# Attention numerators moved into the FFN blocks, down weights streamed per block: a linear-attention plus SwiGLU kernel on one core

## The chip, the cores and the metric

The kernel runs on one core of a Trainium2 chip. The metric is the device time of one execution in microseconds (us). Executions of one kernel agree within 1%. Ratios are the mean time of one kernel's fast runs over that of the other kernel's fast runs of the same rounds, so they are not quite the ratio of the medians quoted beside them. Every "ratio" below is against the kernel before, measured on the same chip.

Words used: TensorE does matmuls, DVE is the vector engine, ScalarE the activation engine, PSUM the memory of the matmul accumulators (the kernels here use eight banks of it, 128 x 512 fp32 each). An "F tile" is a 128-wide slice of the FFN's hidden dimension; there are 36. A "block" is 512 tokens; there are four.

## The reference, cut to what matters

```python
# S = 2048 tokens, D = 576, 32 heads of 18, F = 4608, all bf16
xn  = layernorm(A_x)
q, k, v = heads(xn @ A_wqkv)
phi = lambda t: where(t > 0, t + 1, exp(t)) + 1e-6
kv  = phi(k)^T v          # per head, summed over all tokens
z   = phi(k) summed over tokens
o   = (phi(q) kv) / (phi(q) z + 1e-6)
out = A_x + o @ A_wo + (silu(xn @ B_w_gate) * (xn @ B_w_up)) @ B_w_down
```

Linear attention has one barrier: `kv` and `z` need all tokens before any `o` can be made. The kernel packs them, per group of seven heads, into a small matrix `R` of 126 + 7 columns: multiplying phi(q) by it gives numerators and denominators together.

## The kernel before

Four stages stand in this order: loads and the K/V stage over 16 token tiles; building R; a stage that makes q, numerators and normalised outputs of all tokens; and the FFN with the output projection, block by block. Cuts are marked with `# ...`.

```python
W_DOWN_EARLY_TILES = 6
ATTN_PROJ_AT = 2
ffn_sb = tile_pool(bufs=2)                    # sg, hT (3), ot
ps_x = tile_pool(bufs=3, space=PSUM)          # gate/up banks, shared with the attention "units"
# ... in the attention part: ps_tr 2 banks, ps_y 1, ps_kv 2
wd_a = wpool.tile([P, NFA, D], BF16)          # first 6 down-weight tiles, loaded early

def q_unit(blk, g):                           # phi(q) of one head group for 512 tokens
    pq = pq_buf[blk % 2]
    pu = unit_tile()
    for kt in range(KT):                      # 5 matmuls of 512 columns
        nc.tensor.matmul(pu[0:r, 0:SB], lhsT=wq_sb[...], rhs=xnT[:, kt, bs], ...)
    nc.scalar.activation(a[0:r, :], pu[0:r, 0:SB], ACT.Relu, scale=-1.0)
    nc.scalar.activation(e[0:r, :], a[0:r, :], ACT.Exp, scale=-1.0)
    nc.vector.scalar_tensor_tensor(pq[0:r, g, :], pu[0:r, 0:SB], 0.0, e[0:r, :],
                                   op0=ALU.max, op1=ALU.add)
# K/V stage: the five q units of block 0 are mixed in
early_q = [(0, g) for g in range(NG)]
for i in range(NST):
    transpose_in(i, xn_next)
    # ... layer_norm(i + 1)
    kv_tile(i)
    if i >= TPB and early_q:
        q_unit(*early_q.pop(0))
# ... R is built here
# attention stage: q of the next block, numerators, normalise, transpose, interleaved
for blk in range(NSB):
    for j in range(TPB):
        nd = nd_next
        if blk + 1 < NSB:
            for g in q_share(j):
                q_unit(blk + 1, g)
        # ... nd_next = numden_mm(...)          5 matmuls of 133 columns
        ot = normalize(blk, j, nd)              # DVE: 2 reciprocals, 2 products
        transpose_out(blk, j, ot)               # 5 transposes, one ScalarE copy to oT

def finish_block(blk):
    for j in range(TPB):
        ot = ffn_sb.tile([P, D], BF16, tag="ot")          # two buffers
        nc.vector.tensor_tensor(ot[:, 0:DMAIN], accm[j], xr[...], op=ALU.add)
        nc.vector.tensor_tensor(ot[:, DMAIN:D], acct[:, j, :], xr[...], op=ALU.add)
        nc.sync.dma_start(out2[rows, :], ot[:])
# FFN: per F tile 5 gate, 5 up matmuls, then the down matmuls of the tile before;
# attn_proj(blk) at F tile 2; accumulators take 5 PSUM banks
```

A scheduling layer reorders instructions by priority within the limits of data and buffers, so the order in the trace is near the program's, not equal to it.

## Time and profile before

| | before |
|---|---|
| median of 15 runs | 592.72 us (591.08 to 595.47) |
| profiled span | 592.2 us |
| TensorE busy | 95% |
| first K/V matmul to R | 62.1 us |
| first q unit after R to the last matmul | 507.5 us |
| last matmul to program end | 7.0 us |

The page of the kernel before: busy time and share of each engine, the granted TensorE clock in tenths over 40 slices, and the engines' shares of the chain of work that ended last.

```profile
span 592.2 us, 8308 instructions
...
PE 563.3 (95%) x3472; PEld 280.4 (47%) x3526; DVE 192.2 (32%) x397; ACT 163.5 (28%) x355; POOL 9.3 (2%) x54
...
PEclk7899999899999999999999999999999999999998
...
PE 88%; ACT 4%; DVE 3%; DMA 2%; issue 1%; SPq 1%; DVEq 0%
```

TensorE is the bound: 88% of the chain. (The 95% busy overstates it a little: matmuls overlap and their ends are modelled.) What is left to gain is where TensorE waits, which the stretches view of the same kernel shows. Columns: stretch in us from the start, its length, then busy time and instruction count of each engine, granted clock, DMA share, GB/s.

```profile
core 0: us, PE busy (x) PEld busy (x) DVE busy (x) ACT busy (x) POOL busy (x), PEclk, DMA share, GB/s
13.90:75.98 62.08, 58.57 (x495) 33.32 (x496) 43.88 (x117) 44.83 (x150) 0.16 (x2) 0.96 0.80 230
...
77.68:111.00 33.32, 28.39 (x225) 18.37 (x226) 28.20 (x76) 26.02 (x45) 0.00 (x0) 0.99 0.00 1
111.00:114.97 3.97, 3.75 (x17) 1.82 (x17) 1.23 (x4) 2.47 (x4) 0.00 (x0) 0.62 0.00 0
114.97:585.20 470.23, 467.30 (x2690) 222.73 (x2741) 109.14 (x170) 86.21 (x145) 0.00 (x0) 1.00 0.06 19
585.20:592.20 7.00, 0.00 (x0) 0.00 (x0) 2.36 (x7) 0.00 (x0) 0.00 (x0) 0.73 0.24 84
```

The FFN stretch is full. The attention stage from 77.68 us is not: 4.9 us idle on TensorE up to 111 us, then 4 us at a granted clock of 0.62. Its timeline, TensorE only (start, duration, instruction, count; in brackets the idle time before it and what ended it):

```profile
106.39 0.41 PE L343 MATMUL u<-R,pq 127*128 127x133 bf16 x4 [0.53 <-DVE pq L176]
107.18 0.23 PE L343 MATMUL u<-R,pq 127*128 127x133 bf16 x1 [0.38 <-DVE o L359]
...
109.01 0.28 PE L372 MATMUL pT<-ident,o 128*128 128x128 bf16 x2 [0.56 <-DVE o L359]
...
111.31 1.06 PE L468 MATMUL pg<-xnT,wg_sb 128*128 128x512 bf16 x2 [0.22 <-issue]
112.17 0.42 PE L372 MATMUL pT<-ident,o 128*128 128x128 bf16 x2
112.38 1.06 PE L468 MATMUL pg<-xnT,wg_sb 128*128 128x512 bf16 x2
```

The waits are for DVE: over the whole stage numerators wait 2.0 us for phi(q) (line 176) and transposes 1.8 us for the normalised product (line 359); one numerator waits for that product too (0.38). After them, from 110.6 to 114.0 us, the granted clock reads 0.50.

The end of the program, DVE only:

```profile
585.67 0.34 DVE L455 TENSOR_TENSOR ot<-acct,xr 128x64 bf16<-128x64 f32 x2
587.75 0.69 DVE L451 TENSOR_TENSOR ot<-accm,xr 128x512 bf16<-128x512 f32 x1 [1.74 <-DMA out_dram<-ot]
```

The third addition of the last block waits 1.74 us for an output transfer, because there are two output buffers.

### The profile page before, as it was taken

Reading aid. Unit: us, or ns where it says so; the run is one execution under the profiler, and the core shown is the slowest. Engines: PE = TensorE matmul, PEld = TensorE weight load, DVE = VectorE, ACT = ScalarE, POOL = GpSimd, SP = SyncE. Lnnn points to the kernel's source line nnn. Section 1 sums busy time; section 2 is a strip of 40 time slices with the busy share of each in tenths; the row PEclk is TensorE's granted clock in tenths of the full one; section 3 lists DMA queues with packets and bytes.
Section 4 is the critical chain, followed back from the end, with each engine's and each line's share of the span. In section 5 each row is a group of like instructions: output and inputs, shape, how many; then the busy total and the mean of one; then the engine's idle time right before and its main releaser. Section 6 shows DMA issues by size and latency. Waiting matters only on the chain.

```text
span 592.2 us, 8308 instructions
## 1 busy us (share of the span) xinstructions
PE 563.3 (95%) x3472; PEld 280.4 (47%) x3526; DVE 192.2 (32%) x397; ACT 163.5 (28%) x355; POOL 9.3 (2%) x54
## 2 busy tenths in 40 slices
PE   3999988899999999999999999999999999999995
PEld 2555555444444444444444444444444444444442
DVE  4777488512122223121222141221222412212223
ACT  1777778512212211122112211122122211221120
POOL 6000000000000000000000000000000000000000
PEclk7899999899999999999999999999999999999998
DMA  8999100180000000200000001000000010000001
GB/s 273 329 301 281 31 2 1 53 288 1 0 1 1 1 1 20 61 2 1 0 1 1 0 21 61 1 1 1 0 1 1 24 58 1 0 1 1 1 1 40
DMA packets 19482, 27.59 MB, mean 47 GB/s; under 512 B 1076, under 2 KB 14324, under 8 KB 19444
## 3 DMA queue, kind: packets, MB, share of 16 engines
q1 hardware_dynamic: 19444, 27.06, 15.0%
q8 instruction: 27, 0.44, 0.3%
q14 instruction: 11, 0.09, 0.1%
HBM read 24.70 MB, written 2.36 MB: 46 GB/s over the span
## 4 chain that ended last, share of the span: by engine, by line
PE 88%; ACT 4%; DVE 3%; DMA 2%; issue 1%; SPq 1%; DVEq 0%
PE pu L472 26%; PE pg L468 26%; PE accm L423 23%; PE u L268 5%; PE acct L429 4%; PE u L168 2%; DMA xo<-in_A_x_dram 1%; ACT e L277 1%; ACT a L275 1%; DMA out_dram<-ot 1%; ACT e L175 1%; ACT m L279 1%; DVE ot L451 1%; ACT a L173 1%; PE kvacc L292 1%
## 5 line engine op out<-in xcount | busy, mean ns | idle before, releaser
L477 DVE TENSOR_TENSOR hT<-pu,sg 128x512 bf16<-128x512 f32 x144 | 99.6, 691 | 363.0 <-PE pu L472 360.0
L475 ACT ACTIVATE sg<-pg 128x512 bf16<-128x512 f32 x144 | 86.0, 597 | 381.6 <-PE pg L468 362.9
L472 PE MATMUL pu<-xnT,wu_sb 128*128 128x512 bf16 x709 | 179.1, 379 | 0.8
L468 PE MATMUL pg<-xnT,wg_sb 128*128 128x512 bf16 x702 | 176.9, 381 | 0.9 <-issue 0.2
L423 PE MATMUL accm<-wd_b,hT 128*128 128x512 bf16 x459 | 129.7, 380 | 0.0
L472 PEld LDWEIGHTS <-wu_sb 128*128 128x128 bf16 x720 | 70.2, 98 | 84.1 <-issue 0.7
L429 PE MATMUL acct<-wd_b,hT 128*128 128x64 bf16 x480 | 92.5, 193 | 1.1
L468 PEld LDWEIGHTS <-wg_sb 128*128 128x128 bf16 x720 | 61.0, 98 | 68.5 <-issue 0.3
L423 PEld LDWEIGHTS <-hT 128*128 128x128 bf16 x576 | 56.4, 98 | 68.2 <-DVE hT L477 0.2
L429 PEld LDWEIGHTS <-hT 128*128 128x128 bf16 x576 | 56.0, 98 | 17.5 <-issue 0.4
L268 PE MATMUL u<-wkv_sb,xnT 128*128 128x504 bf16 (+1 forms) x320 | 44.6, 296 | 7.1 <-DVE xnT L256 7.0
L268 PEld LDWEIGHTS <-xnT 128*128 128x128 bf16 x320 | 22.4, 101 | 28.0 <-DVE xnT L256 7.8
L423 PE MATMUL accm<-wd_a,hT 128*128 128x512 bf16 x92 | 26.9, 380 | 0.1
L168 PE MATMUL u<-xnT,wq_sb 128*126 128x512 bf16 (+1 forms) x100 | 24.7, 380 | 0.4 <-DVE pq L176 0.4
L423 PE MATMUL accm<-wo_sb,xo 126*128 126x512 bf16 (+1 forms) x80 | 20.2, 380 | 0.0
L429 PE MATMUL acct<-wd_a,hT 128*128 128x64 bf16 x96 | 17.0, 193 | 0.2
L275 ACT ACTIVATE a<-u 128x504 bf16<-128x504 f32 (+1 forms) x32 | 13.1, 410 | 14.0 <-PE u L268 13.9
L176 DVE SCALAR_TENSOR_TENSOR pq<-u,e 126x512 bf16<-126x512 f32 (+1 forms) x20 | 13.8, 689 | 5.6 <-ACT e L175 4.9
L429 PE MATMUL acct<-wo_sb,xo 126*128 126x64 bf16 (+1 forms) x80 | 15.3, 192 | 0.0
L280 DVE SCALAR_TENSOR_TENSOR pk<-e,m 128x504 bf16<-128x504 bf16 (+1 forms) x32 | 13.1, 451 | 5.8 <-ACT e L277 5.8
L238 DVE BATCH_NORM_STATS2 st<-xo 128x6 f32<-128x288 bf16 x32 | 12.6, 442 | 6.8 <-DMA xo<-in_A_x_dram 6.8
L168 PEld LDWEIGHTS <-wq_sb 128*126 128x126 bf16 (+1 forms) x100 | 11.8, 132 | 6.2 <-issue 0.8
(61 smaller groups left out, 231.1 us busy)
## 6 DMA issues: line engine op xcount, KB each, us to landing
wg_sb<-in_B_w_gate_dram SPq DMA_DIRECT2D x4, 1152.0 KB, 14.6
wu_sb<-in_B_w_up_dram SPq DMA_DIRECT2D x4, 1152.0 KB, 14.9
wd_b<-in_B_w_down_dram SPq DMA_DIRECT2D x5, 864.0 KB, 6.6
xr<-in_A_x_dram SPq DMA_DIRECT2D x4, 576.0 KB, 4.6
out_dram<-ot SPq DMA_DIRECT2D x16, 144.0 KB, 2.2
xo<-in_A_x_dram SPq DMA_DIRECT2D x1, 1152.0 KB, 9.3
wg_sb<-in_B_w_gate_dram SPq DMA_DIRECT2D x8, 144.0 KB, 14.1
wu_sb<-in_B_w_up_dram SPq DMA_DIRECT2D x8, 144.0 KB, 13.4
```

The costliest lines, as they stand in the source:

```text
L168: nc.tensor.matmul(pu[0:r, 0:SB], lhsT=wq_sb[:, kt, g * GW:g * GW + r], rhs=xnT[:, kt, bs], start=(kt == 0), stop=(kt == KT - 1),)
L176: nc.vector.scalar_tensor_tensor(pq[0:r, g, :], pu[0:r, 0:SB], 0.0, e[0:r, :], op0=ALU.max, op1=ALU.add)
L238: nc.vector.bn_stats(st[:, c, :], x_all[:, i, c * BN_CH:(c + 1) * BN_CH])
L268: nc.tensor.matmul(pu[:, 0:w], lhsT=xnT[:, kt, tok], rhs=wkv_sb[:, kt, c0:c0 + w], start=(kt == 0), stop=(kt == KT - 1),)
L275: nc.scalar.activation(a[:, 0:w], pu[:, 0:w], ACT.Relu, scale=-1.0)
L280: nc.vector.scalar_tensor_tensor(pk[:, g0:g1, 0:r], e[:, 0:w].rearrange("p (g c) -> p g c", c=r), PHI_EPS, m[:, 0:w].rearrange("p (g c) -> ...
L423: nc.tensor.matmul(st["accm"][j][:, 0:DMAIN], lhsT=lhsT, rhs=rhs_full[:, 0:DMAIN], start=st["first_main"][j], stop=last,)
L429: nc.tensor.matmul(st["acct"][:, j, :], lhsT=lhsT, rhs=rhs_full[:, DMAIN:D], start=st["first_tail"], stop=last, skip_group_check=True,)
L468: nc.tensor.matmul(pg[:, 0:SB], lhsT=wg_sb[:, kt, fs], rhs=xnT[:, kt, bs], start=(kt == 0), stop=(kt == KT - 1))
L472: nc.tensor.matmul(pu[:, 0:SB], lhsT=wu_sb[:, kt, fs], rhs=xnT[:, kt, bs], start=(kt == 0), stop=(kt == KT - 1))
L475: nc.scalar.activation(sg[:], pg[:, 0:SB], ACT.Silu)
L477: nc.vector.tensor_tensor(hT[:], pu[:, 0:SB], sg[:], op=ALU.mult)
```

## The change

The intent: no stage in which TensorE waits for normalisation. All 20 q units run in one go after R and all phi(q) stay in SBUF; numerators, normalisation and transposes become twelve small steps per block, one in every second F tile of the FFN, where other engines have time. To pay for the memory, the down weights are no longer resident but streamed in chunks of six tiles (three buffers), once per block. PSUM pays too: gate/up have two banks instead of three, and one bank serves the steps. Output buffers go from two to four. The output projection moves from F tile 2 to after the last step (F tile 25). Lines that begin with `#`, here and in the cuts below, stand for code left out.

```diff
-W_DOWN_EARLY_TILES = 6
+W_DOWN_CHUNK = 6
+W_DOWN_BUFS = 3
-ATTN_PROJ_AT = 2
+EPI_START = 1
-    ps_x = ctx.enter_context(tc.tile_pool(name="ps_x", bufs=3, space=PSUM))
+    ps_x = ctx.enter_context(tc.tile_pool(name="ps_x", bufs=2, space=PSUM))
-    wd_a = wpool.tile([P, NFA, D], BF16, name="wd_a")
+    pq_all = [wpool.tile([P, NG, SB], BF16, name=f"pq{b}") for b in range(NSB)]
+    o_buf = [wpool.tile([P, NG, P], BF16, name=f"o{j}") for j in range(2)]
-        ps_y = ... bufs=1 ...
+        ps_y = ... bufs=2 ...
                 kv_tile(i)
-                if i >= TPB and early_q:
-                    q_unit(*early_q.pop(0))
 # ... R is built
-        # the interleaved attention stage
+        for blk in range(NSB):
+            for g in range(NG):
+                q_unit(blk, g)
+        wdp = bctx.enter_context(tc.tile_pool(name="wdp", bufs=W_DOWN_BUFS))
+        ps_att = bctx.enter_context(tc.tile_pool(name="ps_att", bufs=1, space=PSUM))
+        # load_wd(q): one chunk of six down-weight tiles, two chunks ahead
+        # nd_step: 3 or 2 numerator matmuls, reciprocal, product; tr_step: 5 transposes, copy
-                ot = ffn_sb.tile([P, D], BF16, tag="ot")
+                ot = ffn_sb.tile([P, D], BF16, tag="ot", bufs=4)
+        spacing = max(1, (NFT - 6 - f_start) // n_steps)      # 2
                 prev = (blk, f, hT)
-                if f == attn_at:
-                    attn_proj(blk)
+                if pending and f >= f_start:
+                    n_emit = len(pending) if f == NFT - 1 else int((f - f_start) % spacing == 0)
+                    for _ in range(n_emit):
+                        pending.pop(0)()
+                    if not pending:
+                        proj_at = min(NFT - 1, f + 2)
+                if proj_at is not None and f >= proj_at:
+                    attn_proj(blk)
+                    proj_at = None
```

More of the change, by code (lines that the diff above doesn't have):

```diff
@@ L68 @@
     TPB = SB // P
-    NFA = min(W_DOWN_EARLY_TILES, NFT)
-    NFB = NFT - NFA
+    CH = min(W_DOWN_CHUNK, NFT)
+    NCH = (NFT + CH - 1) // CH
     DMAIN = min(D, BANK)
@@ L85 @@
     wu_sb = wpool.tile([P, KT, F], BF16, name="wu_sb")
-    wd_a = wpool.tile([P, NFA, D], BF16, name="wd_a")
     wo_sb = wpool.tile([P, NG, D], BF16, name="wo_sb")
     wq_sb = wpool.tile([P, KT, D], BF16, name="wq_sb")
+    ident = wpool.tile([P, P], BF16, name="ident")
+    R = wpool.tile([P, NG, NDW], BF16, name="R")
+    pq_all = [wpool.tile([P, NG, SB], BF16, name=f"pq{b}") for b in range(NSB)]
+    o_buf = [wpool.tile([P, NG, P], BF16, name=f"o{j}") for j in range(2)]
     def load_ktiled(dst, src, c0, c1, eng, d0=0):
@@ L104 @@
         ps_tr = actx.enter_context(tc.tile_pool(name="ps_tr", bufs=2, space=PSUM))
-        ps_y = actx.enter_context(tc.tile_pool(name="ps_y", bufs=1, space=PSUM))
+        ps_y = actx.enter_context(tc.tile_pool(name="ps_y", bufs=2, space=PSUM))
         ps_kv = actx.enter_context(tc.tile_pool(name="ps_kv", bufs=1, space=PSUM))
@@ L112, in unit_tile @@
             unit_ctr[0] += 1
-            pool, tag = (ps_y, "unit_y") if k % 4 == 3 else (ps_x, "unit")
+            pool, tag = (ps_y, "unit_y") if k % 2 else (ps_x, "unit")
             return pool.tile([P, BANK], F32, tag=tag, name=f"u{k}")
-        ident = apers.tile([P, P], BF16, name="ident")
         make_identity(nc, ident[:])
@@ L127 @@
         Rb = apers.tile([GW, NG, NDW], BF16, name="Rb")
-        R = apers.tile([P, NG, NDW], BF16, name="R")
-        pq_buf = [qpool.tile([P, NG, SB], BF16, name=f"pq{j}", bufs=1) for j in range(2)]
         def init_late_constants():
@@ L149, in init_late_constants @@
             nc.gpsimd.memset(Rb[:], 0.0)
-            for pqj in pq_buf:
+            for oj in o_buf:
+                nc.gpsimd.memset(oj[:, :, GW:P], 0.0)
+            for pqj in pq_all:
                 for g in range(NG):
@@ L164, in q_unit @@
             r = gsz[g]
-            pq = pq_buf[blk % 2]
+            pq = pq_all[blk]
             pu = unit_tile()
@@ L203 @@
                 load_ktiled(wu_sb, B_w_up, c0, c1, nc.sync, d0=c0)
-                if c == 0:
-                    nc.sync.dma_start(
-                        wd_a[:, :, :], B_w_down[0:NFA * P, :].rearrange("(ft p) d -> p ft d", p=P)
-                    )
             for g in range(NG):
@@ L296, in kv_tile @@
                     )
-            early_q = [(0, g) for g in range(NG)]
             xn_next = layer_norm(0)
@@ L304 @@
                 kv_tile(i)
-                if i >= TPB and early_q:
-                    q_unit(*early_q.pop(0))
-            for bg in early_q:
-                q_unit(*bg)
             for g in range(NG):
@@ L325 @@
                 nc.any.tensor_copy(R[0:r + 1, g, :], pr[0:r + 1, 0:NDW])
-        with tc.tile_pool(name="a2", bufs=2) as a2:
-            o_buf = []
-            for j in range(2):
-                oj = a2.tile([P, NG, P], BF16, name=f"o{j}", bufs=1)
-                nc.gpsimd.memset(oj[:, :, GW:P], 0.0)
-                o_buf.append(oj)
-            ND_SPLIT = min(BANK // NDW, NG)
-            nd_parts = [(g0, min(NG, g0 + ND_SPLIT)) for g0 in range(0, NG, ND_SPLIT)]
-            def numden_mm(blk, j):
-                pq = pq_buf[blk % 2]
-                nd = []
-                for (g0, g1) in nd_parts:
-                    t = unit_tile()
-                    for g in range(g0, g1):
-                        r = gsz[g]
-                        nc.tensor.matmul(
-                            t[:, (g - g0) * NDW:(g - g0 + 1) * NDW],
-                            lhsT=pq[0:r + 1, g, j * P:(j + 1) * P], rhs=R[0:r + 1, g, :],
-                            start=True, stop=True,
-                        )
-                    nd.append(t)
-                return nd
-            def normalize(blk, j, nd):
-                i = blk * TPB + j
-                ot = o_buf[i % 2]
-                for (g0, g1), t in zip(nd_parts, nd):
-                    n = g1 - g0
-                    v3 = t[:, 0:n * NDW].rearrange("p (g c) -> p g c", c=NDW)
-                    rden = a2.tile([P, ND_SPLIT, HG], F32, tag="rden")
-                    nc.vector.reciprocal(rden[:, 0:n, :], v3[:, :, GW:NDW])
-                    nc.vector.tensor_tensor(
-                        ot[:, g0:g1, 0:GW].rearrange("p g (h e) -> p g h e", e=Dh),
-                        v3[:, :, 0:GW].rearrange("p g (h e) -> p g h e", e=Dh),
-                        rden[:, 0:n, :].rearrange("p g (h o) -> p g h o", o=1)
-                        .to_broadcast([P, n, HG, Dh]),
-                        op=ALU.mult,
-                    )
-                return ot
-            def transpose_out(blk, j, ot):
-                i = blk * TPB + j
-                pT = ps_tr.tile([P, NG, P], BF16, tag="pT")
-                for g in range(NG):
-                    nc.tensor.transpose(pT[:, g, :], ot[:, g, :], ident[:])
-                nc.scalar.copy(oT[:, :, i * P:(i + 1) * P], pT[:])
-            def q_share(j):
-                return range((NG * j) // TPB, (NG * (j + 1)) // TPB)
-            nd_next = numden_mm(0, 0)
-            for blk in range(NSB):
-                for j in range(TPB):
-                    nd = nd_next
-                    if blk + 1 < NSB:
-                        for g in q_share(j):
-                            q_unit(blk + 1, g)
-                    if j + 1 < TPB:
-                        nd_next = numden_mm(blk, j + 1)
-                    elif blk + 1 < NSB:
-                        nd_next = numden_mm(blk + 1, 0)
-                    ot = normalize(blk, j, nd)
-                    transpose_out(blk, j, ot)
@@ L392 @@
+        for blk in range(NSB):
+            for g in range(NG):
+                q_unit(blk, g)
     with ExitStack() as bctx:
         bp = bctx.enter_context(tc.tile_pool(name="bp", bufs=1))
+        wdp = bctx.enter_context(tc.tile_pool(name="wdp", bufs=W_DOWN_BUFS))
         ps_acc = bctx.enter_context(tc.tile_pool(name="ps_acc", bufs=1, space=PSUM))
-        wd_b = None
-        if NFB:
-            wd_b = bp.tile([P, NFB, D], BF16, name="wd_b")
-            step = 6
-            for f0 in range(0, NFB, step):
-                f1 = min(NFB, f0 + step)
-                nc.sync.dma_start(
-                    wd_b[:, f0:f1, :],
-                    B_w_down[(NFA + f0) * P:(NFA + f1) * P, :].rearrange("(ft p) d -> p ft d", p=P),
-                )
@@ L407, in wd_tile, with load_wd @@
-        def wd_tile(f):
-            return wd_a[:, f, :] if f < NFA else wd_b[:, f - NFA, :]
+        ps_att = bctx.enter_context(tc.tile_pool(name="ps_att", bufs=1, space=PSUM))
+        wd_chunks = {}
+        n_chunks = NSB * NCH
+        def load_wd(q):
+            if q >= n_chunks or q in wd_chunks:
+                return
+            c = q % NCH
+            f0, f1 = c * CH, min(NFT, (c + 1) * CH)
+            t = wdp.tile([P, CH, D], BF16, tag="wd", name=f"wd{q}")
+            nc.sync.dma_start(
+                t[:, 0:f1 - f0, :],
+                B_w_down[f0 * P:f1 * P, :].rearrange("(ft p) d -> p ft d", p=P),
+            )
+            wd_chunks[q] = t
@@ new lines, in wd_tile, with nd_step @@
+        def wd_tile(blk, f):
+            q = blk * NCH + f // CH
+            load_wd(q)
+            return wd_chunks[q][:, f % CH, :]
+        for q in range(min(W_DOWN_BUFS - 1, n_chunks)):
+            load_wd(q)
+        ND_SPLIT = min(BANK // NDW, NG)
+        nd_parts = [(g0, min(NG, g0 + ND_SPLIT)) for g0 in range(0, NG, ND_SPLIT)]
+        def nd_step(blk, j, g0, g1):
+            pq = pq_all[blk]
+            ot = o_buf[(blk * TPB + j) % 2]
+            n = g1 - g0
+            t = ps_att.tile([P, BANK], F32, tag="att", name="nd")
+            for g in range(g0, g1):
+                r = gsz[g]
+                nc.tensor.matmul(
+                    t[:, (g - g0) * NDW:(g - g0 + 1) * NDW],
+                    lhsT=pq[0:r + 1, g, j * P:(j + 1) * P], rhs=R[0:r + 1, g, :],
+                    start=True, stop=True,
+                )
+            v3 = t[:, 0:n * NDW].rearrange("p (g c) -> p g c", c=NDW)
+            rden = ffn_sb.tile([P, ND_SPLIT, HG], F32, tag="rden")
+            nc.vector.reciprocal(rden[:, 0:n, :], v3[:, :, GW:NDW])
+            nc.vector.tensor_tensor(
+                ot[:, g0:g1, 0:GW].rearrange("p g (h e) -> p g h e", e=Dh),
+                v3[:, :, 0:GW].rearrange("p g (h e) -> p g h e", e=Dh),
+                rden[:, 0:n, :].rearrange("p g (h o) -> p g h o", o=1).to_broadcast([P, n, HG, Dh]),
+                op=ALU.mult,
+            )
@@ new lines, in tr_step, with epilogue_steps @@
+        def tr_step(blk, j):
+            i = blk * TPB + j
+            ot = o_buf[i % 2]
+            pT = ps_att.tile([P, NG, P], BF16, tag="att", name="oTp")
+            for g in range(NG):
+                nc.tensor.transpose(pT[:, g, :], ot[:, g, :], ident[:])
+            nc.scalar.copy(oT[:, :, i * P:(i + 1) * P], pT[:])
+        def epilogue_steps(blk):
+            steps = []
+            for j in range(TPB):
+                for (g0, g1) in nd_parts:
+                    steps.append(lambda j=j, g0=g0, g1=g1: nd_step(blk, j, g0, g1))
+                steps.append(lambda j=j: tr_step(blk, j))
+            return steps
@@ L442, in down @@
         def down(blk, f, hT):
+            wd = wd_tile(blk, f)
+            if f % CH == 0:
+                load_wd(blk * NCH + f // CH + W_DOWN_BUFS - 1)
             for j in range(TPB):
-                acc_matmuls(blk, j, hT[:, j * P:(j + 1) * P], wd_tile(f), last=(f == NFT - 1))
+                acc_matmuls(blk, j, hT[:, j * P:(j + 1) * P], wd, last=(f == NFT - 1))
         def finish_block(blk):
@@ L458, in finish_block @@
                 nc.sync.dma_start(out2[rows, :], ot[:])
-        attn_at = min(ATTN_PROJ_AT, NFT - 1)
+        n_steps = TPB * (len(nd_parts) + 1)
+        f_start = min(EPI_START, NFT - 1)
+        spacing = max(1, (NFT - 6 - f_start) // n_steps)
         prev = None
@@ L463 @@
             bs = slice(blk * SB, (blk + 1) * SB)
+            pending = epilogue_steps(blk)
+            proj_at = None
             for f in range(NFT):
@@ L485 @@
                 prev = (blk, f, hT)
-                if f == attn_at:
+                if pending and f >= f_start:
[5 more added lines that the diff above has]
+                if proj_at is not None and f >= proj_at:
                     attn_proj(blk)
+                    proj_at = None
         pb, pf, ph = prev
```

## The prediction

> **What bounds the kernel now.** TensorE: busy 95% of 592.2 us, and the chain of waits lies 88% on it. From the stretches and timeline views:
>
> - First transfers and K/V stage, to 75.4 us. A pair of token tiles takes 8.9 us with two of block 0's q units, 6.6 without: each q unit costs its 1.08 us of TensorE there.
> - 77.7 to 115.0 us: 15 q units (16.2 us of TensorE) interleaved with 80 numerator/denominator matmuls (start to start 0.063 us) and 80 transposes (0.056). With the first gate and up tiles (2.2) that is 28 us of work, so some 9 us are idle or slow. The waits name DVE's normalise and pq writes. At 111 to 114 us gate matmuls start 0.53 us apart instead of 0.216.
> - FFN, to 584.9 us: 3.14 us per F tile, 4.9 us of output projection per block, 117.9 us per block; no loss at block boundaries.
> - Tail: 7.3 us, 1.75 of it additions waiting for an output transfer, as only two output buffers exist.
>
> **What the change does.** TensorE's instruction count is equal. Five q units leave the K/V stage and join 15 others in one run after R. Numerators and transposes (9.5 us of TensorE) move into the FFN, one small step every second F tile, where DVE and ScalarE idle over 2 us per tile; the built order confirms it. Gate/up PSUM drops from 3 to 2 buffers: in steady state silu (0.60) and product (0.69) finish before the buffer is wanted, so no cost. Down weights are streamed again in every block, 16 MB more; an 864 KB chunk landed in 4.7 to 8.3 us, and one is needed per 18.8, so hidden. Output buffers: 2 to 4.
>
> **On the critical path.**
> - K/V stage: -5.4 us.
> - q run: 20 x 1.08 = 21.6 us on TensorE; ScalarE needs about 1.16 per unit, so ends some 3 us later.
> - FFN start, new stall: with two buffers the second gate tile waits for ScalarE's backlog, the 1.28 us table load and silu. The first down chunk shares memory with q temporaries, so its transfer starts after the last pq write, about 25 us after the first q unit, and lands 5 later. First down matmul 30.3 us after the first q unit, where pure work is 27.2: 3 us idle.
> - From first q unit to last matmul: 30.3 + 475.4 (remaining FFN with numerators) = 505.7, against 506.7 before: -1.
> - Tail: -1.7. Boundaries: four additions in a row hold DVE 3.6 us and only two buffers exist: +1 in all.
>
> Sum: about -7 us. The Trainium skill ("TensorE: Matmul & The Clock Gate", Part 1) says the default state is throttled and activity releases it; the 0.53 us matmuls after the gappy stage agree. If the new FFN start throttles too, 1 to 2 us returns.
>
> **Predicted time** 586.5 us, 80% range 582.5 to 591; faster by over 2% 0.06, within 2% 0.91, slower 0.03.
>
> **What would show it right.** R finished near 72 us; no normalise waits before the FFN; the first down matmul waiting for its weight transfer near 100 to 103 us; FFN block period near 120.3 us; matmul end to program end near 5.5 us.
>
> **What would make it wrong.** Numerator steps costing TensorE more than their columns (48 steps); chunks arriving late; boundary stalls; a longer throttle at FFN start; the q run bound harder by ScalarE.

## The result, and the profile after

| | before | after |
|---|---|---|
| median | 592.72 us (15 runs) | 583.30 us (10 runs, 581.68 to 584.85) |
| ratio | | 0.9838, 95% interval 0.9819 to 0.9857 |
| profiled span | 592.2 us | 581.0 us |

The change gains 1.6%, 9.4 us of the medians; the prediction was 586.5 us with a range from 582.5 to 591. All outputs are right. The two profiled executions differ by 11.2 us, more than the medians: that of before lay 1.2 us above its median and that of after 0.6 below.

The page of the changed kernel, the same parts as before:

```profile
span 581.0 us, 8330 instructions
...
PE 558.0 (96%) x3470; PEld 280.7 (48%) x3526; DVE 194.6 (33%) x394; ACT 165.1 (28%) x358; POOL 14.4 (2%) x64
...
PEclk9999999999999999999999999999999999999999
```

The stretches of the changed kernel, cut at its first K/V matmul, the first matmul that builds R, the first q unit after it, the first gate tile, the first down matmul and the last matmul. (Those of before are cut at the same events, except that 111.00 stands just ahead of its first gate tile and 114.97 at its second gate tile.)

```profile
13.62:69.03 55.41, 52.33 (x470) 30.39 (x471) 38.99 (x109) 40.18 (x143) 1.80 (x4) 1.00 0.86 243
...
70.11:91.93 21.82, 21.82 (x104) 13.20 (x104) 11.79 (x18) 20.52 (x39) 0.00 (x0) 1.00 0.01 1
91.93:100.29 8.36, 6.01 (x29) 2.56 (x28) 4.21 (x7) 5.38 (x9) 0.00 (x0) 1.00 0.44 138
100.29:575.94 475.65, 472.75 (x2829) 230.41 (x2884) 130.69 (x230) 95.47 (x158) 0.00 (x0) 1.00 0.17 52
575.94:581.00 5.06, 0.00 (x1) 0.00 (x0) 2.28 (x7) 0.00 (x0) 0.00 (x0) 0.94 0.34 118
```

One clock figure here misleads. The trace of this run holds no clock record before 17.2 us, and the view shows the time without records as 1.00. The first K/V matmuls of 504 columns start 0.42 us apart until 17.2 us and 0.213 after it; in the profile of before they do the same until its record of full clock at 18.4 us. Both K/V stages begin at half speed, the changed one for 3.6 us and that of before for 4.5, so about 0.5 us of the K/V stage's difference in the table below lies in the executions and not in the change.

The 20 q units run without a gap: 21.82 us long, 21.82 us busy. The idle time left is at the start of the FFN. TensorE's timeline there:

```profile
91.93 1.24 PE L460 MATMUL pg<-xnT,wg_sb 128*128 128x512 bf16 x4
94.22 1.24 PE L464 MATMUL pu<-xnT,wu_sb 128*128 128x512 bf16 x5 [1.05 <-DVE pq L179]
95.30 0.35 PE L364 MATMUL nd<-R,pq 127*128 127x133 bf16 x3
96.48 1.24 PE L460 MATMUL pg<-xnT,wg_sb 128*128 128x512 bf16 x5 [0.83 <-ACT sg L467]
...
100.29 0.39 PE L408 MATMUL accm<-wd,hT 128*128 128x512 bf16 x1 [0.41 <-DMA wd<-in_B_w_down_dram]
```

Three waits stand in a row: the first up tile for a PSUM bank that a q unit still holds, the second gate tile for ScalarE's silu, the first down matmul for its weights. The program's end, DVE only, has lost its wait:

```profile
576.42 0.34 DVE L443 TENSOR_TENSOR ot<-acct,xr 128x64 bf16<-128x64 f32 x2
576.68 0.68 DVE L439 TENSOR_TENSOR ot<-accm,xr 128x512 bf16<-128x512 f32 x1
```

Where the 11.2 us of the two profiles lie, from the stretches (us):

| stretch | before | after | difference | predicted |
|---|---|---|---|---|
| start to first K/V matmul | 13.90 | 13.62 | -0.3 | 0 |
| first K/V matmul to R | 62.08 | 55.41 | -6.7 | -5.4 |
| R to first q unit | 1.70 | 1.08 | -0.6 | 0 |
| first q unit to last matmul | 507.52 | 505.83 | -1.7 | -1, boundaries +1 |
| last matmul to end | 7.00 | 5.06 | -1.9 | -1.7 |
| sum | 592.2 | 581.0 | -11.2 | -7 |

This table says where the time went, not why; five fewer q units in the K/V stage, for instance, are paid in a later row. The experiments undo parts of the change one by one.

### The profile page after: what moved, and what is told of

Same layout as the page of the kernel before. It is cut to its first block, busy times and chain, and to the rows that moved or that the text cites. A ratio compares the mean times of both kernels' runs of the same rounds, so it can differ in the third digit from the quotient of the medians.

```text
span 581.0 us, 8330 instructions
## 1 busy us (share of the span) xinstructions
PE 558.0 (96%) x3470; PEld 280.7 (48%) x3526; DVE 194.6 (33%) x394; ACT 165.1 (28%) x358; POOL 14.4 (2%) x64
## 4 chain that ended last, share of the span: by engine, by line
PE 87%; ACT 5%; DVE 3%; DMA 2%; issue 1%; SPq 1%; DVEq 0%
PE pu L464 27%; PE pg L460 26%; PE accm L408 23%; PE acct L414 4%; PE u L171 3%; PE u L267 2%; ACT e L276 1%; ACT a L274 1%; DMA wq_sb<-in_A_wqkv_dram 1%; ACT m L278 1%; DMA wd<-in_B_w_down_dram 1%; PE nd L364 1%; PE oTp L384 1%; DVE pk L279 1%; DVE xnT L255 1%
## 5 line engine op out<-in xcount | busy, mean ns | idle before, releaser
L408 PE MATMUL accm<-wd,hT 128*128 128x512 bf16 x552 | 156.2, 380 | 0.4 <-DMA wd<-in_B_w_down_dram 0.4
L414 PE MATMUL acct<-wd,hT 128*128 128x64 bf16 x576 | 109.5, 193 | 1.3
L171 PE MATMUL u<-xnT,wq_sb 128*126 128x512 bf16 (+1 forms) x100 | 21.9, 379 | 0.0
L385 ACT COPY xo<-oTp 128x640 bf16<-128x640 bf16 x16 | 11.1, 692 | 27.9 <-PE oTp L384 27.9
L179 DVE SCALAR_TENSOR_TENSOR pq<-u,e 126x512 bf16<-126x512 f32 (+1 forms) x20 | 13.8, 691 | 11.3 <-ACT e L178 11.3
L171 PEld LDWEIGHTS <-wq_sb 128*126 128x126 bf16 (+1 forms) x100 | 13.1, 131 | 8.2 <-issue 0.2
L372 DVE TENSOR_TENSOR o<-nd,rden 128x378 bf16<-128x378 f32 (+1 forms) x32 | 15.5, 485 | 1.1
```

What stands on the lines that cost most here:

```text
L171: nc.tensor.matmul(pu[0:r, 0:SB], lhsT=wq_sb[:, kt, g * GW:g * GW + r], rhs=xnT[:, kt, bs], start=(kt == 0), stop=(kt == KT - 1),)
L372: nc.vector.tensor_tensor(ot[:, g0:g1, 0:GW].rearrange("p g (h e) -> p g h e", e=Dh), v3[:, :, 0:GW].rearrange("p g (h e) -> p g h e", e=D ...
L408: nc.tensor.matmul(st["accm"][j][:, 0:DMAIN], lhsT=lhsT, rhs=rhs_full[:, 0:DMAIN], start=st["first_main"][j], stop=last,)
L414: nc.tensor.matmul(st["acct"][:, j, :], lhsT=lhsT, rhs=rhs_full[:, DMAIN:D], start=st["first_tail"], stop=last, skip_group_check=True,)
```

## The experiments

The theory is the prediction's: moving q units is nearly neutral; the gain is waits taken out of the attention stage plus the tail's output wait, less a new stall at the FFN start; two PSUM banks and the streamed weights cost nothing in steady state. Rivals are named with each run. Twelve kernels ran, five rounds each. The control for comparisons with the changed kernel is the changed kernel itself, run again in the second call: 583.32 us, ratio 0.9841 (0.9818 to 0.9864). The kernels are set against this control by their ratios to the kernel before.

> The changed kernel once more, as the control for the other runs of this call. Both theories: ratio 0.982 to 0.986. The clock in the first 30 us is expected to differ from execution to execution (it was 0.79 and 0.85 in the profile of before and 1.0 in that of after); executions whose mean granted clock is 1.0 should be about 2 us shorter than those below.

That held for the ratio. The second half did not hold: among the control's executions at a mean clock of 1.0 were 581.73 and 583.32 us. Its premise was false too. The profile of after has no clock record for its first 17 us, and its matmuls there run at half speed as in the others, so a mean clock of 1.0 does not say that an execution began at full clock.

### Four output buffers in the kernel before

```diff
-                ot = ffn_sb.tile([P, D], BF16, tag="ot")
+                ot = ffn_sb.tile([P, D], BF16, tag="ot", bufs=4)
```

> The kernel before with four output buffers instead of two, nothing else. Theory (the tail gave part of the gain): the 1.74 us in which the last block's additions waited for an output transfer goes, so the time falls by about 1.8 us (ratio near 0.997); last matmul to program end from 7.2 to about 5.4 us; the FFN block period stays 117.9 us. Rival (the output buffers also held up the block boundaries): the block period falls too, and the time by 3 us or more.

590.61 us, ratio 0.9958 (0.9940 to 0.9976): 2.5 us by the ratio. In the profile the time from last matmul to end fell from 7.0 to 5.2 us, and the block period was 117.90 us against 117.99. The theory held: in the kernel before, the buffers are a matter of the tail.

### Two output buffers in the changed kernel

```diff
-                ot = ffn_sb.tile([P, D], BF16, tag="ot", bufs=4)
+                ot = ffn_sb.tile([P, D], BF16, tag="ot")
```

> The changed kernel with two output buffers again. Theory: last matmul to program end 5.4 to 7.2 us, +1.8 us against the control; block boundaries may cost up to 1 us more each, because the next product on DVE now stands behind two waits for output transfers with only two gate/up buffers in PSUM. Rival (output buffers do nothing for the change): within 0.5 us of the control.

588.74 us, ratio 0.9934 (0.9914 to 0.9955): 5.4 us more than the control. The tail took 1.8 us of it. The rest came at the block boundaries, three times, and once by more than the 1 us that was expected at most (1.7, 1.0 and 1.0): block to block, the first outputs stood 121.92, 121.21 and 119.32 us apart, against 120.26, 120.25 and 118.29. So the same edit is worth 2.5 us in the kernel before and 5.4 in the changed one. Read the other way: with four output buffers in both kernels all the rest of the change gains about 7 us (ratios 0.9958 and 0.9841), with two in both about 4. DVE at the first boundary of this run:

```profile
220.74 0.55 DVE L372 TENSOR_TENSOR o<-nd,rden 128x378 bf16<-128x378 f32 x1
223.10 0.69 DVE L439 TENSOR_TENSOR ot<-accm,xr 128x512 bf16<-128x512 f32 x1 [1.82 <-DMA out_dram<-ot]
...
224.76 0.69 DVE L439 TENSOR_TENSOR ot<-accm,xr 128x512 bf16<-128x512 f32 x1 [0.83 <-DMA out_dram<-ot]
```

DVE waits twice for an output to land, the accumulators stay occupied, and TensorE waited 0.7 and 0.6 us there for them. The SP queue of the same run at this boundary (start, duration of issuing) shows what is new:

```profile
217.57 0.37 SPq L340 DMA_DIRECT2D wd<-in_B_w_down_dram  x1
218.12 7.82 SPq L446 DMA_DIRECT2D out_dram<-ot  x4
```

An 864 KB weight chunk is issued 0.55 us ahead of the outputs on the same queue. The first output, issued at 218.12, released its buffer at about 223.1, 5 us later and 0.44 us after the chunk had landed (222.64). The trace holds the landing of eight of the run's 16 outputs: 1.7 us at the least, 1.8 in the median and 5.1 at the worst. The three long ones (4.7 to 5.1) were issued within 1.3 us of a chunk; two later outputs at the boundaries, issued more than 6 us after a chunk, took 1.7 and 1.8. In the kernel before, which has no chunk there, the worst was 3.1, and 3.9 in two of its variants. The Trainium skill ("DMA: Bandwidth & Descriptors", "Queues, rings and completion order") says that each DMA engine takes descriptors of a queue in ring order; outputs standing behind the chunk agree with that, and the worst landing is close to the chunks' own median of 4.7.

### The two PSUM banks alone, in the kernel before

```diff
-    ps_x = ... bufs=3 ...
+    ps_x = ... bufs=2 ...
-        ps_y = ... bufs=1 ...
+        ps_y = ... bufs=2 ...
-            pool, tag = (ps_y, "unit_y") if k % 4 == 3 else (ps_x, "unit")
+            pool, tag = (ps_y, "unit_y") if k % 2 else (ps_x, "unit")
```

> The kernel before with the PSUM split of the change: two gate/up buffers instead of three, the other buffer given to the attention units. Theory (two buffers suffice in steady state): FFN block period 117.9 us as before, the time within 0.3%, at most 1.5 us longer at the start of the FFN. Rival (the third buffer was worth something, and the change pays for it): block period at least 0.3 us longer, more than 1.5 us in all.

594.36 us, ratio 1.0028 (1.0006 to 1.0050): 1.7 us longer. The block period is 117.99 us, as before to the hundredth; R to the first down matmul grew from 41.15 to 42.74 us. The theory held for the steady state: two banks cost nothing there. The 1.6 us before it is slightly more than the 1.5 expected, and most of it lies elsewhere than expected: 1.35 us of it passes before the first gate matmul, in the attention stage, where TensorE's waits of numerators for phi(q) grew from 2.0 to 3.6 us. At the FFN start a wait of 0.9 us for the first silu is new. This run also has two output buffers and two gate/up banks, and no boundary stall. DVE at its first boundary:

```profile
236.38 0.69 DVE L477 TENSOR_TENSOR hT<-pu,sg 128x512 bf16<-128x512 f32 x1 [0.99 <-PE pu L472]
236.98 0.68 DVE L451 TENSOR_TENSOR ot<-accm,xr 128x512 bf16<-128x512 f32 x1
```

The third addition starts 2.3 us after the first output was issued (234.69) and waits for nothing. So the boundary stall of the run before this one does not come from two PSUM banks and two output buffers alone. (This run lacks both the weight chunk and the numerator steps there, so it does not tell these two apart.)

### Requesting the weight chunk later

```diff
-            if f % CH == 0:
+            if f % CH == 3:
                 load_wd(blk * NCH + f // CH + W_DOWN_BUFS - 1)
```

> The changed kernel with two output buffers, and the next down-weight chunk requested at the fourth F tile of a chunk instead of its first, so that no chunk is in flight when a block's outputs are written. In the run with two output buffers alone the block periods were 121.92, 121.21 and 119.32 us against 120.26, 120.25 and 118.29, and the first output of a block boundary took up to 5.1 us to land. Theory (the streamed chunk delays the output, and the output holds the buffer): outputs land in about 2.2 us, block periods return to 120.3 us (within 0.3), only the tail's 1.8 us stay; ratio 0.986 to 0.989. Rival (two gate/up buffers in PSUM make the boundary stall, whatever the outputs take): periods stay near 121.5 us, ratio 0.992 to 0.995.

588.67 us, ratio 0.9930 (0.9913 to 0.9947), and the same block periods. But the run tests nothing: the chunk's transfer was still issued at 217.45 us, 0.54 us ahead of the outputs. Here the scheduling layer issued it when the last reader of its buffer was done, at the block boundary, although the program asked for it later. The rival is not confirmed by it either. That the chunk in flight delays the outputs is therefore read from the traces (about 5 us for outputs issued just behind it, 1.7 to 3.9 in the kernels without), not shown by an experiment.

### Block 0's q units out of the K/V stage, in the kernel before

```diff
                 kv_tile(i)
-                if i >= TPB and early_q:
-                    q_unit(*early_q.pop(0))
             for bg in early_q:
                 q_unit(*bg)
```

> The kernel before with block 0's five q units taken out of the K/V stage and run right after it. Theory (the move of the q units is only a move): the K/V stage ends about 6.3 us earlier, the run of five units pays 5.4 us back, net between -1 and 0 us. Rival (the shorter K/V stage is the gain): the time falls by 5 us or more.

591.08 us, ratio 0.9963 (0.9945 to 0.9982): 2.2 us less. Neither expectation was met; the move is worth more than the theory's 1 us at most and much less than the rival's 5. The last accumulation of K/V comes 54.2 us after its first matmul and R 5.0 us later, against 60.6 and 1.0 in the kernel with four output buffers, whose K/V stage begins at half speed for about as long (3.5 us, here 3.2): the five units (5.4 us of matmuls) partly fill the waits before R, and inside the K/V stage each of them had cost more than its matmuls.

### Block 0's q units back in the K/V stage, in the changed kernel

```diff
                 kv_tile(i)
+                if i >= TPB and i - TPB < NG:
+                    q_unit(0, i - TPB)
...
-        for blk in range(NSB):
+        for blk in range(1, NSB):
```

> The changed kernel with block 0's five q units put back into the K/V stage. Theory: the K/V stage is about 6.3 us longer, the q run 5.4 us shorter, FFN period and tail unchanged: 0 to +1.2 us against the changed kernel (ratio to before 0.984 to 0.987). Rival (the shorter K/V stage is the gain): most of the gain is lost, ratio above 0.992.

583.63 us, ratio 0.9850 (0.9828 to 0.9871): 0.3 us above the changed kernel's median, ratio 0.001 higher. First K/V matmul to R took 61.8 us instead of 55.4, R to the first down matmul 25.8 instead of 31.3. The theory held: the large number in the second row of the table above is mostly a move.

### All steps of a block at once

```diff
-                    n_emit = len(pending) if f == NFT - 1 else int((f - f_start) % spacing == 0)
+                    n_emit = len(pending)
```

> The changed kernel with all twelve numerator and transpose steps of a block emitted together at its second F tile instead of one every second tile. Theory (the gain is that each step's round trip through DVE or ScalarE is hidden under FFN matmuls): with one attention PSUM bank the steps chain through DVE and ScalarE, about 1.2 us each, so part of the waits return: some 1 to 4 us per block, block period 121 to 124 us, ratio 0.99 to 1.01. Rival (it is enough that the steps stand in the FFN at all, the scheduler fills in): block period 120.3 us, ratio as the control.

585.88 us, ratio 0.9878 (0.9857 to 0.9898): 2.6 us more than the control. The block period is 120.99 us, 0.74 more. The run lies between the two expectations. Spacing matters, but less than expected: the scheduling layer puts FFN matmuls between the steps, and only 0.8 us of TensorE's idle time in the whole run is put down to the copies on ScalarE. Of the 0.74 us per block 0.3 is idle time in the trace; the rest stands as busy time and is not explained. The spacing is thus worth 2.6 of the 9.4 us. The other 7 contain the output buffers, the q run and the shorter waits together, and this run does not tell them apart.

### The stall at the FFN start

Three versions. The first shortens ScalarE's part of a q unit from two activations to one: exp(min(x, 0)) equals min(exp(x), 1).

```diff
-            nc.scalar.activation(a[0:r, :], pu[0:r, 0:SB], ACT.Relu, scale=-1.0)
+            nc.scalar.activation(a[0:r, :], pu[0:r, 0:SB], ACT.Exp)
-            nc.scalar.activation(e[0:r, :], a[0:r, :], ACT.Exp, scale=-1.0)
+            nc.vector.tensor_scalar(e[0:r, :], a[0:r, :], 1.0, None, op0=ALU.min)
```

The second gives the residual tile two buffers, only to shift the weight chunks in memory away from the q temporaries, so that the first chunk need not wait for the last q unit. (In its trace the chunk is issued at 70.9 us, against 95.4 in the changed kernel.)

```diff
-            xr = bp.tile([P, TPB, D], BF16, name="xr")
+            xr = bp.tile([P, TPB, D], BF16, name="xr", bufs=2)
```

The third does both.

> The changed kernel with only the q units' ScalarE work shortened (one exp, clamp on DVE). First q unit to first down matmul was 30.2 us in the changed kernel and 26.9 us with both edits. Theory (two waits behind each other, ScalarE's backlog and the first weight chunk): the backlog goes, but the chunk still waits for the last q unit, about 23.5 us after the first, and lands 4.9 us later: 28.3 to 29 us, so 1.2 to 2 us gained of 3.3. Rival (ScalarE alone was the wait): 26.9 us, as with both.

> The changed kernel with only the first weight chunk moved off the q temporaries. Theory: the chunk lands long before it is wanted, but the second gate tile still waits for ScalarE's backlog and table load: first q unit to first down matmul 29.7 to 29.9 us, so 0.3 to 0.5 us gained, not visible in the time. Rival (the chunk was the wait): 28 us or less.

> The changed kernel with both causes of the new stall at the FFN start taken away: in the q units ScalarE does one exp, and the clamp is a min on DVE (the same function, exp of min(x,0) as min of exp(x) and 1), so ScalarE keeps no backlog; and x's residual tile has two buffers, which moves the first down-weight chunk off the memory of the q temporaries, so it can load right after the K/V stage. Theory: first q unit to first down matmul 30.2 to about 28 us, 1.5 to 2.5 us less in all than the control. Rival (the stall is set by the clock or by issue): no change.

| | median, us | ratio | first q unit to first output, us |
|---|---|---|---|
| changed kernel (control) | 583.32 | 0.9841 | 147.65 |
| chunk moved | 582.90 | 0.9832 (0.9807 to 0.9857) | 147.17 |
| one activation | 581.19 | 0.9802 (0.9782 to 0.9823) | 146.24 |
| both | 580.53 | 0.9791 (0.9769 to 0.9814) | 145.50 |

The expectations were written for the first down matmul, 30.1 us after the first q unit in the control. It came at 28.5 (chunk moved), 28.5 (one activation) and 26.9 us (both). That turned out a bad marker: in the two kernels with the chunk moved the scheduling layer put the first down tile before the third gate tile instead of after it, 1.08 us of work earlier. So 28.5 for the chunk alone, taken as it stands, misses its expectation of 29.7 to 29.9; with the 1.08 added it is 29.6. By the first output, which has the same work before it in all four, the gains are 0.5, 1.4 and 2.2 us. ScalarE's backlog was the longer of the waits and the chunk stood behind it: moving the chunk gains 0.5 us alone and 0.7 once the backlog is gone. In the time of the whole run the chunk's part is within the noise. The theory holds in this form, and the rival of a stall set by clock or issue falls. TensorE at the FFN start with both:

```profile
93.95 1.24 PE L464 MATMUL pu<-xnT,wu_sb 128*128 128x512 bf16 x5
95.03 0.34 PE L364 MATMUL nd<-R,pq 127*128 127x133 bf16 x3
95.63 1.24 PE L460 MATMUL pg<-xnT,wg_sb 128*128 128x512 bf16 x5 [0.25 <-ACT sg L467]
96.95 1.24 PE L464 MATMUL pu<-xnT,wu_sb 128*128 128x512 bf16 x5
98.02 0.38 PE L408 MATMUL accm<-wd,hT 128*128 128x512 bf16 x1
```

The waits for pq and for the weights are gone; what is left is ScalarE's table load before the first silu.

### A version that beats both

Both edits, and block 0's five q units between the K/V stage and the building of R, which the run with late q units suggested.

```diff
+            for g in range(NG):
+                q_unit(0, g)
             for g in range(NG):
                 # ... R of group g
-        for blk in range(NSB):
+        for blk in range(1, NSB):
```

> The version with both edits at the FFN start, and block 0's five q units placed between the K/V stage and the building of R, so that they fill the waits of that chain (0.7 us before the last accumulation, 0.65 us before R, in the changed kernel). Theory: 1 to 1.8 us less than the version with both edits, ratio 0.976 to 0.979. Rival (the moved units cost as much as they fill): same as that version, 0.979 or more.

579.15 us, ratio 0.9769 (0.9746 to 0.9791), the fastest kernel here. Against the version with both edits it is 1.4 us by the medians; the intervals of the two ratios overlap, so this last step is likely, not settled.

## Why the prediction was right

The measured 583.3 us lie in the predicted range, near its lower end. Point by point:

- **K/V stage, -5.4 predicted.** Undersized. First K/V matmul to R takes 61.6 us in the kernel before with four output buffers and 55.4 in the changed kernel, whose half-speed starts are about as long (3.5 and 3.6 us): -6.2. Twelve of the fourteen profiles give the same: with h the time from the first K/V matmul to the record of full clock (3.4 to 6.0 us), the stretch is 53.6 us + h/2 in the eight profiles of the changed kernel and its variants with the same K/V stage, and 59.8 us + h/2 in the four with q units in it, each within 0.02 us. The prediction had measured 8.9 against 6.6 us per pair of tiles, 2.3 for two q units, and then booked the 1.08 us of matmuls per unit instead of that 1.15; the rest are small waits (TensorE idles 3.5 and 3.1 us in the two stretches). A further 0.6 us between R and the first q unit went too, since numerators no longer stand between R's matmuls.
- **First q unit to first down matmul, 30.3 predicted.** 30.2 measured, with the waits that were foreseen: PSUM and ScalarE's backlog, the table load, the weight chunk (issued at 95.39, right after the last pq write ended at 95.31, and waited for until 100.29).
- **The rest of the FFN, 475.4 predicted.** 475.65 measured; block period 120.25 us, 120.3 predicted. The 48 steps cost TensorE their columns and nothing more, and the streamed chunks were never late after the first.
- **Boundaries, +1 predicted.** 0 measured: this term failed. The prediction let four additions in a row on DVE hold up the two gate/up banks; with four output buffers the block period is that of the pure sum. What does cost time there, with two buffers, is the wait for outputs to land, 3.6 us in all, and the prediction had not seen it: it counted four output buffers only as 1.7 us of tail, and in the changed kernel they are worth 5.4. That the change brought four of them is luck from the prediction's side.
- **Tail, -1.7 predicted.** -1.9.
- **Throttle.** The prediction left open whether the new FFN start would be throttled. It was not: the granted clock there is 1.00 in all ten profiles of the changed kernel and its variants, against 0.62 in the last 4 us of the attention stage of before, and a like drop (a mean of 0.89 from 104 to 120 us) in the three variants of before. By the clock alone that is an estimate of 1.5 us (3.97 x 0.38), on the gain's side. The Trainium skill ("TensorE: Matmul & The Clock Gate", Part 1) says the default state is throttled and activity releases it; the gappy stage and its slow end agree, the gapless q run and its full clock too. No threshold comes out of it: in the profile of before TensorE is busy 2.2 of the 3.4 us before the drop, but also only 2.1 of the 3.4 us from 73.05, after which the clock stays at 1.00.

The prediction stood 3.2 us above the median. Its own terms sum to -7.1 us, which would be 585.6; the other 0.9 us up to 586.5 are presumably its allowance for a throttled FFN start, which did not come. The three misses that count (K/V stage 0.8, the step after R 0.6, boundaries 1.0) have one sign and make up the rest.

Not resolved: of the 9 us that the attention stage of before took beyond its work, 4.8 are waits in the trace and about 1.5 the clock; some 3 us remain between the estimate of pure work and the trace. And no run separates the move of the numerators from all else: the changed kernel's gain with two output buffers was 3.9 us, with four 9.4, so the parts do not simply add.

## What to carry to other kernels

Work that waits on a chain through other engines is best cut into small steps and put into a stage where the bounding engine is saturated and the others idle; it then costs its own matmul time only, here 48 steps at no visible extra. Count what the move changes at the seams, because the gain is decided there: one gate/up bank fewer cost 1.7 us in the old kernel, and two more output buffers were worth 2.5 us there and 5.4 in the changed one. When several waits stand in a row, measure up to a point that has the same work before it in every version, and expect a later one to show in full only after the one before it is gone. And before a clock of 1.00 at the start of a profile is believed, look at how far apart the first matmuls start.

## What the Trainium skill lacked or had wrong

The first point rests on ScalarE's timeline of the changed kernel at the FFN start:

```profile
93.89 0.63 ACT L178 ACTIVATE e<-a 72x512 bf16<-72x512 bf16 x1
94.54 1.28 ACT L467 ACT_TABLE_LOAD   x1
95.83 0.60 ACT L467 ACTIVATE sg<-pg 128x512 bf16<-128x512 f32 x1
```

- "ScalarE: Activation LUTs", "What ACT_TABLE_LOAD costs", gives 1283 ns for the load plus about 1380 ns of drain, 2.66 us for every switch of set. The load took 1.28 us here, but no drain shows: from the end of the last exp (94.52) to the first silu (95.83) it is 1.31 us in all.
- "DMA: Bandwidth & Descriptors" has the ring order, from which such a delay could be foreseen, but none of its rules for authors warns that a small store issued just behind a large prefetch on the same queue can hold its buffer for the prefetch's time: 144 KB outputs landed in up to 5.1 us with an 864 KB chunk issued 0.55 us ahead of the first of them, against 1.7 to 1.9 us with nothing in front. (Read from traces; the run meant to test it did not move the chunk.)
- "TensorE: Matmul & The Clock Gate", Part 1, gives the cold state "after ≥1 idle window (~3.4µs)". The runs agree: TensorE idles 5.0 to 7.4 us before the first K/V matmul, and in all fourteen profiles these matmuls start 0.42 us apart for their first 3.2 to 6.0 us, 0.213 afterwards. What the page lacks is how the clock's record can mislead there. It calls such events unreliable in general, but not that they can be missing at the start: in ten of the fourteen profiles the first record stands at 16.3 to 20.8 us, and the views show the time before it as 1.00.
